# Attention with 49 agents and a maxout layer: a written-out order exchanged up to group 22, key values in pairs of chunks, five relu slots

## The chip, the cores and the metric

The kernel runs on one core of one Trainium2 chip. The metric is the time of one execution on the device, in microseconds (us), as the median of several runs. The core has five engines with an instruction stream each: PE (TensorE, matrix products), ACT (ScalarE), DVE (VectorE), POOL (GpSimd) and SP (SyncE, which here issues DMA transfers alone). Each works through its stream strictly in order. Transfers that SP issues form one queue, which sixteen DMA engines serve.

## The reference

Two layers follow each other. The first is attention through 49 agents: the agents gather from all keys and values of a batch, and each query then reads from the agents. The second is a maxout layer with three weight matrices and a product back to 128 columns.

```python
def _attn_ref(q, k, v, agents):          # q, k, v: 4 x 12544 x 128, agents: 4 x 49 x 128
    scale = 1.0 / np.sqrt(q.shape[-1])
    def sm(a, b):
        s = scale * (a @ b.transpose(0, 2, 1))
        ...
        return e / (e.sum(-1, keepdims=True) + 1e-09)
    a2k = sm(agents, k)
    agent_v = a2k @ v
    q2a = sm(q, agents)
    return q2a @ agent_v
def _moe_ref(x, w1, w2, w3, w_out):      # x: 50176 x 128, w1..w3: 128 x 768, w_out: 768 x 128
    h = np.maximum(np.maximum(x @ w1, x @ w2), x @ w3)
    return h @ w_out
```

## The kernel before, in words

**The algebra.** The output of the attention is never formed. For each batch the agents' values (49 x 128) are multiplied once by differences of the weights (w3-w1, w2-w1) and by w1 times w_out, into a table G of the batch (`gp`, `gv`). A row of the hidden layer then is a product of the 49 exponentials of a query with G, and the maximum of three becomes a relu of one difference (u), a maximum with the other (v), and a linear part (li) that goes straight to the output. The division by the sum of the exponentials comes last, when the output is scaled.

**Batches and groups.** There are 98 tiles of 128 rows per batch. Keys and values are taken in chunks of up to nine tiles (`chunks`, L175); queries in groups of eight tiles, 1024 rows: 12 groups a batch and one made of what remains, 49 in all (`parts_of`, L168). Batch 0's keys and values must be done before group 0, those of batch 1 before group 12, of batch 2 before group 24, of batch 3 before group 36. Chunks of the next batch are worked off between the groups.

**The steps**, by the names of the order (`graph`, L208):

- Chunk g of batch b: `kl`, `vl` load keys and values (SP), `kc`, `vc` cast them to bf16 (POOL; in batch 0 `vc` is on ACT), `kt` turns the keys (by PE and a copy `ke` on DVE in batch 0, by a transposing DMA on SP's queue later, L283), `ks` are the scores (PE, L285), `kx` the exponentials (ACT), `kv` the values (PE), `va` their sum (DVE), `ea` the sum of the exponentials (POOL).
- Group s: `ql` loads queries (SP), `qc` casts them (POOL). They are turned either by PE with a copy on DVE (`qt`, `qe`) or by a transposing DMA on SP's queue (`qd`); the list TURNED (L26) says which groups take the DMA (L318). `sc` are the scores (PE), `ex` the exponentials (ACT). For each of six parts f of the hidden layer: `u` (PE), `a` the relu (ACT), `v` (PE), `x` the maximum (DVE); for part 4 both are on ACT. `li` and `p` are the products into the output (PE; ROWS says for each part whether the 128 rows are taken as a whole or in two halves that run side by side), `su` and `re` the sums and their reciprocals, `ov` the scaling (DVE, or ACT where SCALER says so), `st` the store (SP).

**What sets the order.** No scheduler runs when the kernel is built. ORDER (L826) is a string of step names that was written out beforehand; `Emit.run` walks it once, and each engine's stream is its steps in that order. A number behind a name is the slot that a new tile takes in its pool (SLOTS, L46): 13 buffers for loads (LD), 3 each for cast queries and keys (QB, KB), 4 for turned ones (QT, KT), 3 for relus (AS), 13 for hidden parts (R), 10 for outputs (OS), 8 banks of PSUM (PS). `Plan.waits` works out from the order which step waits for which, a step that takes over a slot waiting for those that used it. All steps go through one recording helper, so that every row of the profile has that helper's line, L388; the rows are told apart by tile names.

Of the kernel before, what the change touches and what calls it, by code (L numbers as in the profile page):

```python
# [9 lines left out]
FP32 = mybir.dt.float32  # L10
# [9 lines left out]
C31, C21, C1O, WC = 0, DFF, 2 * DFF, 2 * DFF + C  # L20
CV, CT = KT * A, (KT - 1) * A
FI = 4
SPARE = 8
FIRST = [KT] * 10 + [4, 4]
LATER = [KT] * 10 + [8]
TURNED = (10, 13, 15, 18, 22, 24, 25, 28, 29, 30, 31, 32, 33, 34, 35, 36, 37, 38, 39, 40, 41, 42, 43, 44, 45, 46, 47, 48,)  # L26
ROWS = """
rrfrff rrrffr ffrfff ffrfrr rfffff rrrrrr ffffff ffffrr fffrff rfrrfr fffffr ffrfrf rrfrrr fffffr fffffr frffrf fffrrr rfffff
ffffff rrrfff ffffrf rrrfff rrffrr ffrrrr rrrrrr ffffff ffffff rrfffr ffrfrr rrrrrr ffffff ffffff fffffr rffrfr rrrrrr ffrffr
# [3 lines left out]
...... u..... .u.... ...... ...... ...... ...... ...... ...... ...... .u.u.. uu.... ...... ...... ...... ...u.. ..u... ......  # L33
...... ...... ...... .u.... ...... ...... ..u... ..u..u ...... ...... ...... ...... ..u... ...... ...... ...... ...... ......
...... ...... ...... ...... ...... ...... ...... ...... u..... ...... ...... ...... ......
""".split()
SCALER = """
dd dd dd dd dd dd dd dd dd dd dd dd dd dd dd dd dd dd dd dd dd dd ad dd dd dd dd dd dd dd dd dd dd dd dd dd dd dd dd dd dd dd dd
# [16 lines left out]
class Plan:  # L55
# [104 lines left out]
    def lane(self, o, place, first):  # L160
        if not o["use"]:
            return "AG"
# [45 lines left out]
def graph(plan, em):  # L208
# [3 lines left out]
    add("id0", POOL, em.clear_ident, (0.3, 0.6))  # L212
    add("id", POOL, em.make_ident, (0.3, 0.6), after=["id0"])
    add("ones", DVE, em.make_ones, (1.0, 1.1), after=["id0"])
    add("agl", ACT, em.load_agents, (0.5, 5.0), dma=True)
    add("agc", DVE, em.cast_agents, (0.42, 0.52), after=["agl"])
    add("agt", PE, em.turn_agents, (0.2, 0.4), after=["agc", "id"], new=[("PS", "agt")])
# [23 lines left out]
    for g in range(len(ch)):  # L241
        add(f"wn.{g}", PE, em.warm(f"warn.{g}", 2), (0.445, 0.67), after=["id", f"vl0.{g}"], new=[("PS", f"warn.{g}")])
# [812 lines left out]
```

## Time and profile before

| | |
|---|---|
| runs | 438.46, 439.33, 439.44 us (median 439.33) |
| profiled execution: span from first to last instruction | 436.6 us |
| PE busy | 411.9 us, 6488 matmuls |
| DVE busy | 386.6 us, 470 instructions |
| ACT busy | 393.9 us, 486 instructions |
| POOL busy | 170.0 us |
| moved by DMA | 122.37 MB, mean 280 GB/s |

The span starts with the first instruction of any engine. The runs' median is 2.7 us over the span; what lies around the span isn't in the profile. PE's busy time is modelled, since matmuls overlap in the array, and a busy PE isn't one at its peak. In a row of a window the busy times come in the order PE, PEld (loading of weights), DVE, ACT, POOL, then the clock granted to PE, the share of time that the sixteen DMA engines were at work (over 1 where packets overlap), and the rate. In rows for one tile a name stands for all buffers of its pool: QT is turned queries, KT turned keys, LD loads, R hidden parts, AS relus, VA sums of values, OS outputs, agT the agents. "DMA to landing" is from the start of SP's instruction to the arrival of the transfer's last completion.

### The profile page before, as it was taken

The page shows a single profiled execution, that of the slowest core. Times are in us where ns is not written, and L with a number is a line of the kernel's source. Part 1 is how long each engine was busy: PE and PEld are TensorE (multiplying, and loading weights), DVE is VectorE, ACT ScalarE, POOL GpSimd, SP SyncE. Part 2 cuts the span into 40 slices and gives each one's busy share as a digit, 9 for nine tenths or more (in the row PEclk, how much of TensorE's full clock was granted, in tenths as well). Part 3 has the DMA queues.
Part 4 walks back from the last instruction along what each step waited for, and adds up shares of the span by engine and source line. Part 5 has one row for each costly group of instructions (what it writes and reads, how often), then busy time and mean ns, then how long its engine had stood idle before and what let it go on. Part 6 is the DMA issues. An engine that isn't in the chain of part 4 may idle for free.

```text
span 436.6 us, 14853 instructions
## 1 busy us (share of the span) xinstructions
PE 411.9 (94%) x6488; PEld 256.9 (59%) x6488; DVE 386.6 (89%) x470; ACT 393.9 (90%) x486; POOL 170.0 (39%) x177
## 2 busy tenths in 40 slices
PE   1788999999999999999999999999999999999994
PEld 1464565666666566656656655656656555655574
DVE  1435999999999999999998999899999999999994
ACT  1278999999999999999999899999999999999993
POOL 3541565556655535165525445342531111000000
PEclk9989999999999999999999999999999999999999
DMA  8999999999999999999999999996999994266313
GB/s 310 411 410 383 311 334 372 289 281 343 269 318 342 279 371 298 266 339 285 294 345 261 407 247 278 276 326 143 276 363 290 284 306 98 74 208 208 119 71 125
DMA packets 98107, 122.37 MB, mean 280 GB/s; under 512 B 71479, under 2 KB 74235, under 8 KB 98043
## 3 DMA queue, kind: packets, MB, share of 16 engines
q1 hardware_dynamic: 97552, 121.07, 95.2%
q8 instruction: 51, 0.84, 0.8%
q10 hardware_dynamic: 491, 0.36, 0.3%
q14 instruction: 13, 0.11, 0.1%
HBM read 78.74 MB, written 25.69 MB: 239 GB/s over the span
## 4 chain that ended last, share of the span: by engine, by line
PE 69%; ACT 16%; DVE 7%; DMA 4%; issue 2%; POOL 1%; SPq 0%; POOLq 0%
PE ps L388 69%; ACT AS L388 9%; DVE R L388 6%; DMA LD<-in_k_dram 4%; ACT R L388 2%; ACT ps L388 2%; POOL KB L388 1%; DVE OS L388 1%; ACT EQ L388 1%; ACT VB L388 1%; ACT G L388 1%; ACT EK L388 1%; ACT OS L388 0%; SPq L388 0%; DVE QT L388 0%
## 5 line engine op out<-in xcount | busy, mean ns | idle before, releaser
L388 DVE TENSOR_TENSOR R<-ps,AS 128x1024 bf16<-128x1024 f32 x245 | 293.5, 1219 | 15.1 <-PE ps L388 10.7
L388 ACT ACTIVATE AS<-ps 128x1024 bf16<-128x1024 f32 (+1 forms) x259 | 245.8, 987 | 10.0 <-PE ps L388 7.2
L388 PE MATMUL ps<-EQ,G 49*128 49x512 bf16 (+1 forms) x1248 | 203.3, 370 | 3.5 <-ACT AS L388 0.7
L388 PE MATMUL ps<-wo_bf,R 64*128 64x128 bf16 (+1 forms) x3368 | 194.0, 218 | 1.1 <-issue 0.8
L388 PEld LDWEIGHTS ps<-wo_bf,R 64*128 64x128 bf16 (+1 forms) x3368 | 139.5, 95 | 59.4 <-issue 31.3
L388 PEld LDWEIGHTS ps<-EQ,G 49*128 49x128 bf16 x1248 | 56.4, 93 | 63.8 <-DVE R L388 18.3
L388 POOL CAST QB<-LD 128x1024 bf16<-128x1024 f32 x49 | 50.5, 1040 | 94.6 <-DMA QT<-QB 49.8
L388 POOL CAST KB<-LD 128x1152 bf16<-128x1152 f32 (+2 forms) x45 | 49.8, 1115 | 52.1 <-DMA LD<-in_k_dram 41.8
L388 DVE TENSOR_TENSOR OS<-ps,RC 128x512 f32<-128x512 f32 x96 | 65.4, 682 | 2.6 <-PE ps L388 2.2
L388 POOL CAST VB<-LD 128x1152 bf16<-128x1152 f32 (+1 forms) x33 | 37.4, 1136 | 40.7 <-DMA LD<-in_v_dram 36.5
L388 ACT ACTIVATE ps<-ps 128x1024 f32<-128x1024 f32 x49 | 49.9, 1018 | 2.8 <-PE ps L388 2.2
L388 ACT ACTIVATE R<-ps 128x1024 bf16<-128x1024 f32 x49 | 50.3, 1027 | 1.9 <-PE ps L388 1.6
L388 ACT ACTIVATE EK<-ps 128x441 bf16<-128x441 f32 (+2 forms) x45 | 23.4, 535 | 18.8 <-PE ps L388 18.4
L388 POOL TENSOR_TENSOR EA<-EA,EK 128x441 f32<-128x441 f32 x27 | 27.6, 1022 | 25.4 <-ACT EK L388 25.1
L388 ACT ACTIVATE EQ<-ps 128x512 bf16<-128x512 f32 x49 | 29.9, 610 | 1.0 <-PE ps L388 0.5
L388 DVE COPY KT<-ps 128x1152 bf16<-128x1152 bf16 (+1 forms) x12 | 8.2, 701 | 14.0 <-PE ps L388 14.0
L388 PE MATMUL ps<-QT,agT 128*64 128x512 bf16 (+1 forms) x104 | 19.9, 388 | 0.2
L388 PE MATMUL ps<-G,EQ 49*128 49x128 bf16 x392 | 19.1, 217 | 0.0
L388 PE MATMUL ps<-EK,VB 128*128 128x49 bf16 x392 | 17.4, 186 | 1.6 <-ACT VB L388 1.6
L388 PEld LDWEIGHTS ps<-EK,VB 128*128 128x128 bf16 x392 | 13.9, 97 | 8.1 <-ACT EK L388 4.2
L388 PE MATMUL ps<-agT,KT 128*128 128x49 bf16 x392 | 17.4, 186 | 0.4 <-DVE KT L388 0.4
L388 PEld LDWEIGHTS ps<-agT,KT 128*128 128x128 bf16 x392 | 14.4, 98 | 4.7 <-issue 2.1
(59 smaller groups left out, 177.6 us busy)
## 6 DMA issues: line engine op xcount, KB each, us to landing
LD<-in_q_dram SPq DMA_DIRECT2D x48, 512.0 KB, 7.7
out_dram<-OS SPq DMA_DIRECT2D x48, 512.0 KB, 6.2
LD<-in_k_dram SPq DMA_DIRECT2D x40, 576.0 KB, 7.6
LD<-in_v_dram SPq DMA_DIRECT2D x40, 576.0 KB, 8.4
LD<-in_k_dram SPq DMA_DIRECT2D x3, 512.0 KB, 5.3
LD<-in_v_dram SPq DMA_DIRECT2D x3, 512.0 KB, 6.7
LD<-in_moe_w_dram SPq DMA_DIRECT2D x6, 192.0 KB, 10.6
KT<-KB SPq DMA_TRANSPOSE x33, 7.3
```

The lines of the kernel that those rows point to most:

```text
L388: i = call(*args, **named)
```

## The change

- ORDER is another one up to group 22. From the middle of group 22's products on, the engines' streams are the old ones, with other slots; some casts and stores that stood behind the join stand ahead of it.
- Batch 0 is cut into twelve chunks of eight tiles and one of two, its values are loaded into output buffers and cast on ACT, POOL or DVE (VCAST), its exponentials lie in R slots, sums and values have a PSUM bank each. The weights' loads are cut into three parts each, and the products for G of batch 0 accordingly (CUTS, PARTS).
- The queries of groups 20, 21 and 23 are turned by DMA (TURNED).
- `u` can be evacuated in two halves as before, and now `v` too (SPLIT: u, v, or b for both). Up to group 22 there are 24 more halves of relus and 41 more of maxima than before.
- `kv` takes two chunks at a time into a bank of its own, and `va` adds once per pair.
- AS has five slots instead of three.
- The linear part of G has 256 columns, a half for each side, with zeros beside it, copied in two pieces. (LINEAR could take it in two products; it is "b" throughout, which is the old way.)

```diff
-FIRST = [KT] * 10 + [4, 4]
+FIRST = [GT] * 12 + [2]
-TURNED = (10, 13, 15, 18, 22, 24, 25, 28, 29, 30, ...
+TURNED = (10, 13, 15, 18, 20, 21, 22, 23, 24, 25, 28, 29, 30, ...
 SPLIT = """
-...... u..... .u.... ...... ...... ...... ...... ...... ...... ...... .u.u.. uu.... ...... ...... ...... ...u.. ..u... ......
+v.v..b vbvv.. v.u..v uv.... .....v uv.v.u ..v... .b.u.v v.vb.b .uuv.. uu.u.u vvb..v ..bv.u .....b ubv... .vbu.. uvb..v .v.b.u
...
-SLOTS = {"PS": 8, "LD": 13, "QB": 3, "KB": 3, "VB": 4, "KT": 4, "QT": 4, "EQ": 4, "EK": 4, "AS": 3,
+SLOTS = {"PS": 8, "LD": 13, "QB": 3, "KB": 3, "VB": 4, "KT": 4, "QT": 4, "EQ": 4, "EK": 4, "AS": 5,
...
-            add(f"kv{r}", PE, em.values(b, g, n, m), mm(n, 49), after=[f"kx{r}", f"vc{r}"], use=[m, f"vb{r}", f"e{r}"])
-            add(f"va{r}", DVE, em.add_values(b, g, m), (0.13, 0.25), after=[f"kv{r}"] + ([f"va{b}.{g - 1}"] if g else []),
-                use=[m, plan.tile("VA", f"va{b}")])
+            if g % 2 or g == len(ch) - 1:
+                two = [(x, ch[x][1]) for x in range(g // 2 * 2, g + 1)]
+                y, h = f"{b}.{g // 2}", f"y{b}.{g // 2}"
+                add(f"kv{y}", PE, em.values(b, two, h), mm(sum(x[1] for x in two), 49), after=[f"{z}{b}.{x}" for x, _ in two for z in ("kx", "vc")],
+                    new=[("PS", h)], use=[f"{z}{b}.{x}" for x, _ in two for z in ("vb", "e")])
+                add(f"va{y}", DVE, em.add_values(b, g // 2, h), (0.13, 0.25), after=[f"kv{y}"] + ([f"va{b}.{g // 2 - 1}"] if g > 1 else []),
+                    use=[h, plan.tile("VA", f"va{b}")])
...
+                if SPLIT[s][f] in "vb":
+                    vs = [f"{v}.{h}" for h in range(2)]
+                    add(v, PE, em.hidden(vs, s, f, C21, True), pe, mode=ROW, after=[f"ex.{s}"] + needs(1), new=[("PS", x) for x in vs],
+                        use=[e] + gs)
+                    for h in range(2):
+                        add(f"x.{s}.{f}.{h}", DVE, em.max_second(vs[h], s, f, h), (0.6, 0.72), after=[v, f"{a}.{h if SPLIT[s][f] == 'b' else 0}"],
+                            use=[vs[h], a, r])
```

ORDER itself is a table of some 2900 names; at three places its effect on the streams is shown. First SP's stream around the transposition for group 22, before. In it OS are stores, LD loads of q, k or v, QT turned queries, KT turned keys; from above, the QT row is group 22, the two KT rows chunks 9 and 10 of batch 2, the stores those of groups 9, 17 and 15.

```order
L388 DMA LD_88<-in_q_dram 128x1024
L388 DMA out_dram<-OS_143 128x1024
L388 DMA LD_84<-in_k_dram 128x1152
L388 DMA LD_82<-in_v_dram 128x1152
L388 DMA_TRANSPOSE KT_102<-KB_96 128x9x128
L388 DMA LD_80<-in_v_dram 128x1024
L388 DMA_TRANSPOSE QT_106<-QB_91 128x8x128
L388 DMA out_dram<-OS_144 128x1024
L388 DMA LD_85<-in_q_dram 128x1024
L388 DMA out_dram<-OS_140 128x1024
L388 DMA_TRANSPOSE KT_101<-KB_94 128x8x128
```

SP's stream at that place now: from above, the four QT rows are groups 20, 21, 22 and 23, the KT rows chunks 10, 7 and 9 of batch 2, the store that of group 4.

```order
L416 DMA LD_77<-in_v_dram 128x1152
L416 DMA_TRANSPOSE QT_101<-QB_88 128x8x128
L416 DMA_TRANSPOSE KT_97<-KB_91 128x8x128
L416 DMA_TRANSPOSE KT_99<-KB_92 128x9x128
L416 DMA_TRANSPOSE QT_104<-QB_87 128x8x128
L416 DMA_TRANSPOSE KT_98<-KB_90 128x9x128
L416 DMA_TRANSPOSE QT_102<-QB_89 128x8x128
L416 DMA_TRANSPOSE QT_103<-QB_88 128x8x128
L416 DMA LD_75<-in_v_dram 128x1152
L416 DMA out_dram<-OS_139 128x1024
```

Three of the four transposed query tiles are new on this queue; seven transpositions stand one behind another.

The second place is SP's stream at the store of group 1 (the row with OS_136 now). Before, that store (OS_141) stood behind the transposition of chunk 3.1 (the KT row on top).

```order
L388 DMA_TRANSPOSE KT_102<-KB_95 128x9x128
L388 DMA LD_84<-in_v_dram 128x1152
L388 DMA out_dram<-OS_143 128x1024
L388 DMA LD_90<-in_q_dram 128x1024
L388 DMA LD_85<-in_q_dram 128x1024
L388 DMA LD_83<-in_v_dram 128x1152
L388 DMA out_dram<-OS_141 128x1024
```

Now it stands between loads for batches 1 and 2 (group 15's queries on top, chunk 2.0's keys at the bottom). The store of group 13 moved too, from behind chunk 3.8's transposition to ahead of chunk 2.7's load of keys; all other stores that stood ahead of chunk 3.1's transposition still do.

```order
L416 DMA LD_77<-in_q_dram 128x1024
L416 DMA LD_78<-in_k_dram 128x1152
L416 DMA LD_76<-in_q_dram 128x1024
L416 DMA LD_81<-in_v_dram 128x1152
L416 DMA LD_79<-in_q_dram 128x1024
L416 DMA out_dram<-OS_136 128x1024
L416 DMA LD_80<-in_k_dram 128x1152
L416 DMA LD_83<-in_k_dram 128x1152
```

The third place is PE's stream at the scores of group 20 (the row with agT and QT). Before, the queries were turned by eight products with the unit matrix (ident) some rows ahead.

```order
L388 MATMUL ps<-ident,QB_93 128x128 x8
L388 MATMUL ps<-EK_114,VB_99 128x49 x9
L388 MATMUL ps<-wo_bf,R_121 128x128 x4
L388 MATMUL ps<-wo_bf,R_128 128x128 x4
L388 MATMUL ps<-EQ_112,G_148 128x512 x6
L388 MATMUL ps<-G_148,EQ_109 128x128 x8
L388 MATMUL ps<-wo_bf,R_128 128x128 x4
L388 MATMUL ps<-wo_bf,R_122 128x128 x8
L388 MATMUL ps<-EQ_112,G_148 128x512 x6
L388 MATMUL ps<-QT_105,agT 64x512 x2
```

Now no such row stands there, and the values (EK and VB) of two chunks follow each other.

```order
L416 MATMUL ps<-EK_112,VB_95 128x49 x9
L416 MATMUL ps<-EK_111,VB_93 128x49 x9
L416 MATMUL ps<-EQ_108,G_146 128x512 x2
L416 MATMUL ps<-G_146,EQ_107 128x128 x8
L416 MATMUL ps<-EQ_108,G_146 128x512 x2
L416 MATMUL ps<-wo_bf,R_126 128x128 x4
L416 MATMUL ps<-wo_bf,R_122 128x128 x4
L416 MATMUL ps<-wo_bf,R_127 128x128 x4
L416 MATMUL ps<-EQ_108,G_146 128x512 x4
L416 MATMUL ps<-wo_bf,R_122 128x128 x4
L416 MATMUL ps<-QT_101,agT 64x512 x2
```

PE and DVE lose the turning of groups 20, 21 and 23; the scores of group 25 stand behind the same products in both orders.

More of the change, by code (lines that the diff above doesn't have):

```diff
@@ L331, in graph, with needs @@
         for f in range(NF):
-            def needs(first, second):
+            def needs(second):
                 out = []
                 for p in parts:
-                    out.append(f"gv{first if f < 3 else second}" + (str(p[0]) if p[0] else ""))
+                    if p[0]:
+                        out.append(f"gv{'abcd'[second * 2 + f // 3]}{p[0]}")
+                    else:
+                        out.append(f"gv{'abcdef'[second * 3 + (f > 0) + (f > 2)]}0")
                 return out
-            e, u, v, r, two = f"e.{s}", f"u.{s}.{f}", f"v.{s}.{f}", plan.tile("R", f"r.{s}.{f}"), SPLIT[s][f] == "u"
+            e, u, v, r = f"e.{s}", f"u.{s}.{f}", f"v.{s}.{f}", plan.tile("R", f"r.{s}.{f}")
@@ new lines, in graph @@
+                add(f"a.{s}.{f}.0", ACT, em.relu(u, u, None), (0.917, 1.076), after=[u], use=[u])
+                add(v, PE, em.hidden([u], s, f, C21, False), pe, mode=ROW, after=[f"a.{s}.{f}.0"] + needs(1), use=[u, e] + gs)
+                if SPLIT[s][f] == "d":
+                    add(f"x.{s}.{f}.0", DVE, em.relu(r, u, None, DVE), (1.14, 1.28), after=[v], use=[u, r])
+                else:
+                    add(f"x.{s}.{f}.0", ACT, em.relu(r, u, None), (0.917, 1.076), after=[v], use=[u, r])
@@ L344, in graph @@
             else:
                 a = plan.tile("AS", f"a.{s}.{f}")
-                if two:
+                if SPLIT[s][f] in "ub":
                     us = [f"{u}.{h}" for h in range(2)]
-                    add(u, PE, em.hidden(us, s, f, C31, True), pe, mode=ROW, after=[f"ex.{s}"] + needs("a", "b"), new=[("PS", x) for x in us],
+                    add(u, PE, em.hidden(us, s, f, C31, True), pe, mode=ROW, after=[f"ex.{s}"] + needs(0), new=[("PS", x) for x in us],
                         use=[e] + gs)
@@ L352, in graph @@
                 else:
-                    add(u, PE, em.hidden([u], s, f, C31, True), pe, mode=ROW, after=[f"ex.{s}"] + needs("a", "b"), new=[("PS", u, 3)], use=[e] + gs)
-                    add(a, ACT, em.relu(a, u, None), (0.917, 1.076), after=[u], use=[u, a])
-                add(v, PE, em.hidden([v], s, f, C21, True), pe, mode=ROW, after=[f"ex.{s}"] + needs("c", "d"), new=[("PS", v, 3)], use=[e] + gs)
-                add(f"x.{s}.{f}", DVE, em.max_second(v, s, f), (1.14, 1.28), after=[v] + ([f"{a}.{h}" for h in range(2)] if two else [a]),
-                    use=[v, a, r])
@@ L358, in graph @@
-        lin = ["gvl" if p[0] == 0 else f"gvl{p[0]}" for p in parts]
+                    add(u, PE, em.hidden([u], s, f, C31, True), pe, mode=ROW, after=[f"ex.{s}"] + needs(0), new=[("PS", u, 3)], use=[e] + gs)
+                    add(f"{a}.0", ACT, em.relu(a, u, None), (0.917, 1.076), after=[u], use=[u, a])
+                if SPLIT[s][f] in "vb":
[5 more added lines that the diff above has]
+                            use=[vs[h], a, r])
+                else:
+                    add(v, PE, em.hidden([v], s, f, C21, True), pe, mode=ROW, after=[f"ex.{s}"] + needs(1), new=[("PS", v, 3)], use=[e] + gs)
+                    add(f"x.{s}.{f}.0", DVE, em.max_second(v, s, f, None), (1.14, 1.28), after=[v] + [f"{a}.{h}" for h in range(1 + (SPLIT[s][f] == "u"))],
+                        use=[v, a, r])
@@ L463, in clear_ident, with clear_linear @@
         self.nc.gpsimd.memset(self.sides, 0.0)
+    def clear_linear(self):
+        for i in range(SLOTS["G"]):
+            self.nc.gpsimd.memset(self.slots["G", i][:, C1O:], 0.0)
     def make_ident(self):
```

644 lines of the change are left out of this document (341 added, 303 removed).

## The prediction

> **What bounds the kernel now.** I read the page's slices first (part 2), where all four of PE, DVE, ACT and DMA look full, then the groups, then stretches by window, then single transfers. The first view is the page's slices of 10.9 us each: busy tenths of DVE and ACT, the granted clock, the DMA engines' share and the rate.
>
> ```profile
> DVE  1435999999999999999998999899999999999994
> ACT  1278999999999999999999899999999999999993
> DMA  8999999999999999999999999996999994266313
> GB/s 310 411 410 383 311 334 372 289 281 343 269 318 342 279 371 298 266 339 285 294 345 261 407 247 278 276 326 143 276 363 290 284 306 98 74 208 208 119 71 125
> ```
>
> From slice 4 to slice 34 ACT and DVE stand at nine tenths, and so do the DMA engines, though the rate wanders between 143 and 411 GB/s. A queue that is full at 300 GB/s has something in it that is not measured in bytes. Three windows show what: the first two hold one query transposition each, the third plain loads.
>
> ```profile
> 255.00:257.20 2.20, 2.20 (x26) 1.14 (x24) 2.20 (x5) 2.05 (x3) 2.20 (x3) 1.00 1.14 136
> 288.10:290.30 2.20, 2.20 (x60) 1.64 (x56) 2.20 (x3) 2.06 (x3) 0.32 (x1) 1.00 1.36 131
> 107.00:109.30 2.30, 2.30 (x22) 1.02 (x22) 2.19 (x3) 2.30 (x4) 2.02 (x2) 1.00 1.04 410
> ```
>
> The columns are PE, PEld, DVE, ACT and POOL busy time, clock, DMA share and GB/s. While a transposition runs, the sixteen engines are over 100% busy and move 131 to 136 GB/s, 0.29 to 0.30 MB in 2.2 us; the tile itself is 128x1024 bf16, 0.26 MB, so 0.03 to 0.04 MB (0.1 us at 410) is other traffic: 2.1 us for one, in which almost nothing else moves. A load or store of 128x1024 f32 (0.524 MB) costs 0.524/0.410 = 1.28 us.
>
> A long stretch checks both prices: the number of transpositions issued between 60 and 280 us (by tile name), and the window over the same time.
>
> ```profile
> L388 SPq DMA_TRANSPOSE KT<-KB x28: 1248/2811/6979, 59.3 to 275.9; - x28
> L388 SPq DMA_TRANSPOSE QT<-QB x11: 1237/2894/6058, 102.6 to 272.8; - x11
> 60.00:280.00 220.00, 218.75 (x3444) 136.42 (x3438) 208.87 (x253) 209.74 (x262) 116.57 (x118) 1.00 1.11 309
> ```
>
> 220 us at 309 GB/s are 68.0 MB. The 39 transposed tiles hold about 11.1 MB of it (0.29 MB a key tile, 0.26 a query tile). The other 56.9 MB take 138.8 us at 410; 81.2 us are left for 39 transpositions, 2.08 each. Both prices hold together only if the DMA engines had no pause in 220 us, and their share of 1.11 says the same. So up to 280 us a transfer lands when the work ahead of it on SP's queue is done, and anything added ahead makes it later, one for one. DVE and ACT have 11.1 and 10.3 us of idle time in those 220 us.
>
> What the engines lose by this is read from single transfers: issue (last times of the row), issue to landing, and the first matmul that reads the tile on PE. First group 25's queries.
>
> ```profile
> L388 SPq DMA_TRANSPOSE QT<-QB x1: 6058/6058/6058, 221.8 to 221.8; - x1
> DMA to landing us min/median/max: 12.1/12.1/12.1
> ...
> L388 PE MATMUL ps<-QT,agT x2: 403/403/403, 237.6 to 237.6; 128*64 128x512 bf16 x2
> ```
>
> Landed at 233.9, read at 237.6: 3.7 us to spare. Then chunk 1 of batch 3's keys, chunk 0 of batch 2's, and chunk 9 of batch 3's.
>
> ```profile
> L388 SPq DMA_TRANSPOSE KT<-KB x1: 3035/3035/3035, 233.0 to 233.0; - x1
> DMA to landing us min/median/max: 6.2/6.2/6.2
> ...
> L388 PE MATMUL ps<-agT,KT x9: 183/183/197, 242.9 to 243.2; 128*128 128x49 bf16 x9
> ```
>
> ```profile
> L388 SPq DMA_TRANSPOSE KT<-KB x1: 2497/2497/2497, 116.5 to 116.5; - x1
> DMA to landing us min/median/max: 7.7/7.7/7.7
> ...
> L388 PE MATMUL ps<-agT,KT x8: 183/183/197, 134.5 to 134.7; 128*128 128x49 bf16 x8
> ```
>
> ```profile
> L388 SPq DMA_TRANSPOSE KT<-KB x1: 1445/1445/1445, 300.5 to 300.5; - x1
> DMA to landing us min/median/max: 3.2/3.2/3.2
> ...
> L388 PE MATMUL ps<-agT,KT x9: 183/183/187, 306.8 to 307.0; 128*128 128x49 bf16 x9
> ```
>
> To spare: 242.9-239.2 = 3.7 us, 134.5-124.2 = 10.3, 306.8-303.7 = 3.1. The queue does not show in the chain of waits because the order leaves these few microseconds; it is the second bound, 3.7 us behind the compute engines at groups 24 and 25.
>
> **The change, part by part.** The sum goes against the profiled span, 436.6 us; the median of the runs is 439.33, so 2.7 us lie around the span.
>
> *Three more transpositions, and stores that go ahead.* The queries of groups 20, 21 and 23 leave PE and DVE for SP's queue: 3 x 2.1 = 6.3 us of queue. In the order, the stores of groups 1 and 13 now stand before the transposition for group 25 and that for chunk 3.1; before they stood behind both: 2 x 1.28 = 2.6 us. All else ahead of these two places is the same loads, in bytes. So both land 8.9 us later: 242.8 and 248.1 instead of 233.9 and 239.2. Less the 3.7 us to spare, PE meets them 5.2 us later than before, whatever the engines did until then. PE takes its instructions in order: behind the scores of group 25 (sc.25) stand the hidden layer of group 24 and the output of 23, on these ACT and DVE wait, and on them the rest of the program, which keeps its old order. The price of one query transposition lies between 1.9 (the 81.2 us shared out by tile size, a query tile being 8/9 of a key tile) and 2.3 (the whole 2.2 us of a window and a tenth for the hand-over); I take 2.1, what the windows give: 5.2 becomes 4.6 to 5.8 at the ends.
>
> The other places: ahead of chunk 2.0 stand five key and value loads (0.59 MB each) and one query load that stood behind it: 3.5 MB, 8.5 us, so it lands at 132.7 where it was read at 134.5. So already in group 11 the new order cannot be more than 1.8 us ahead of the old one. At chunk 3.9 only the three transpositions remain: 6.3-3.1 = 3.2 us late, less than the 5.2 already lost.
>
> *Start.* The last values of batch 0 and their cast on ACT:
>
> ```profile
> L388 SPq DMA_DIRECT2D LD<-in_v_dram x2: 432/432/432, 27.2 to 27.6; - x2
> ...
> DMA to landing us min/median/max: 9.4/9.9/10.4
> ...
> 38.47 1.16 ACT L388 ACTIVATE VB<-LD 128x1152 bf16<-128x1152 f32 x1
> ```
>
> They land at 27.6+10.4 = 38.0 and ACT casts them 0.4 us later. The new order has the same 12.8 MB and one q load ahead of them at the same rate, and casts on POOL, ACT and DVE. Gain: 0.5 us, between 0 and 1.5 (the cast and the 0.3 us for the weights' first part). It is gone at chunk 2.0.
>
> *Work of ACT and DVE up to group 22.* The rows for it, from the groups by shape:
>
> ```profile
> L388 DVE TENSOR_TENSOR R<-ps,AS 128x1024 bf16<-128x1024 f32 x245 | 293.5, 1219 | 15.1 <-PE ps L388 10.7 <-ACT AS L388 1.2
> L388 ACT ACTIVATE AS<-ps 128x1024 bf16<-128x1024 f32 x231 | 230.9, 1033 | 7.8 <-PE ps L388 5.2
> L388 DVE TENSOR_TENSOR OS<-ps,RC 128x512 f32<-128x512 f32 x96 | 65.4, 682 | 2.6 <-PE ps L388 2.2
> L388 ACT ACTIVATE AS<-ps 128x512 bf16<-128x512 f32 x28 | 15.4, 604 | 2.2 <-PE ps L388 2.0
> L388 DVE COPY QT<-ps 128x1024 bf16<-128x1024 bf16 x21 | 14.3, 683 | 1.4 <-PE ps L388 1.4
> L388 DVE TENSOR_TENSOR VA<-ps,VA 128x49 f32<-128x49 f32 x30 | 5.9, 197 | 0.3
> ```
>
> ACT splits 24 more relus in two: 24 x (2 x 0.604-1.033) = +4.2 us. DVE splits 41 maxima; the nearest row for a half is the 128x512 product at 0.682: 41 x (1.364-1.219) = +5.9; it loses three evacuations (-2.0) and ten sums of values, by pairs (-2.0). So +4 on ACT, +2 on DVE, against idle time of 11.1 and 10.3 us in 220, or 9.1 and 8.4 in the 180 us from 60 to 240: -8 to +4 in all, and I take 0, because the queue decides first. The halves free PSUM banks sooner; ACT's row shows its waits ended by PE, not by DVE, so five relu slots instead of three take away nothing that stands there: 0.
>
> *Behind group 22* the engines' order is the old one. A typical stretch there:
>
> ```profile
> 320.00:360.00 40.00, 39.29 (x640) 23.36 (x638) 38.91 (x44) 39.16 (x47) 8.27 (x8) 1.00 1.12 304
> ```
>
> DVE and ACT are 97 and 98% busy, so lost time isn't won back. Five sums of values go (5 x 0.197 = 1.0 us on DVE), the linear part is copied in two pieces: 0, at most -1.5.
>
> Sum: 436.6+5.2 = 441.8 of span, with 2.7 around it **444.5 us**.
>
> [...]
>
> **The rivals.** *Faster: the order pays and the queue gives way.* Half of DVE's and ACT's idle time from 60 to 240 us goes (9.1 and 8.4, so -4.4), and the start gives -0.5: 439.3-4.9 = 434.4. It decides if the transfer for group 25 lands before 229, which needs room in the queue that the share of 1.11 denies; for it speaks that landing times were read in one execution. Chance 0.13.
>
> *Much slower: the stop costs clock.* Two stretches of the start show what a waiting PE does.
>
> ```profile
> 24.00:28.00 4.00, 2.36 (x51) 2.04 (x49) 0.51 (x2) 2.64 (x4) 2.10 (x2) 0.88 1.02 408
> 28.00:32.00 4.00, 4.00 (x53) 2.75 (x51) 1.23 (x3) 2.70 (x6) 1.56 (x3) 0.69 1.03 413
> ```
>
> PE was busy for 59% of four microseconds, and the clock fell to 0.88 and 0.69. The same after the stops at groups 24 and 25 would take (0.12+0.31) x 4 = 1.7 us each, 3.4: 447.9, and a little more if the queue also runs dry behind a wait. PE is not the tightest engine, which speaks against. Chance 0.17. [...]
>
> *No change: a transposition costs its bytes.* Beside other transfers it would then take 0.26/0.41 = 0.64 us, three 1.9, with the stores 4.5, less 3.7 to spare: 0.8 late, 440.1. The 81.2 us left over for 39 of them speak against it. Chance 0.07.
>
> **How the numbers follow.** The forecast has 0.63 and reaches from 442 to 447: 4.6 to 5.8, less 1.5 or plus up to 1.5 for the split work. Faster has 0.13, no change 0.07, slower 0.63+0.17 = 0.80; 0.2% (0.9 us) is about what the measurement can tell. The range reaches down over the no-change case to 440 and up to 449; outside lie the faster case and the far end of the slowest.
>
> **What would show it.** In the new profile: sc.25 and the keys of chunk 3.1 read some 243 and 248 us from the start, right at their landing, with PE, ACT and DVE idle ahead of them and the idle time put down to a DMA into QT or KT; DMA share still above 1 up to there. The forecast is wrong if these are read before 238, or if they land that late and the end still comes by 440.

## The result, and the profile after

| | median | lowest to highest | runs |
|---|---|---|---|
| after | 440.85 us | 438.87 to 443.53 | 6 |
| before, beside it | 438.41 us | 437.85 to 439.44 | 6 |

The ratio is 1.0052, 95% interval [1.0031, 1.0074]: slower by 2.4 us, where 5.2 were forecast. The profiled execution took 440.69 us; its span is 438.6. First the page's slices, as those shown of before.

```profile
DVE  1434999999999999999899999899999999999994
ACT  1255999998999999999999899999999999999994
DMA  7999999999999999999999989999699992256313
GB/s 274 413 410 374 306 291 378 240 412 234 356 396 215 348 410 257 345 259 290 417 313 294 387 238 271 286 261 269 203 335 274 320 277 74 75 160 239 134 60 136
```

Counted from 0, no slice of DVE or ACT from 4 to 38 falls under eight tenths: the stop that was forecast for slices 21 and 22 (230 to 252 us) isn't there. Next two single transfers on which the forecast stood: first the queries of group 25 in the profile of after, their issue, landing and first matmul.

```profile
L416 SPq DMA_TRANSPOSE QT<-QB x1: 3107/3107/3107, 226.6 to 226.6; - x1
...
DMA to landing us min/median/max: 8.3/8.3/8.3
...
L416 PE MATMUL ps<-QT,agT x2: 403/403/403, 238.6 to 238.6; 128*64 128x512 bf16 x2
```

They landed at 226.6+8.3 = 234.9 and were read 3.7 us later. Chunk 1 of batch 3's keys, in the same way:

```profile
L416 SPq DMA_TRANSPOSE KT<-KB x1: 2820/2820/2820, 234.7 to 234.7; - x1
...
DMA to landing us min/median/max: 6.3/6.3/6.3
...
L416 PE MATMUL ps<-agT,KT x9: 183/183/198, 243.9 to 244.1; 128*128 128x49 bf16 x9
```

Landed at 241.0, read at 243.9, 2.9 us to spare. So two landings that were to come 8.9 us later came 1.0 and 1.7 us later, and nothing waited for them. (Chunk 2.0 landed at 133.9 and was read 1.2 us later.)

The same stretch of the queue, from 45 us to the landing of group 25's queries, in before and in after:

```profile
45.00:234.00 189.00, 187.59 (x2932) 116.53 (x2932) 180.38 (x221) 180.55 (x226) 101.89 (x103) 1.00 1.11 312
```

```profile
45.00:235.00 190.00, 187.44 (x2856) 115.35 (x2855) 182.21 (x253) 182.81 (x255) 102.46 (x105) 1.00 1.09 321
```

In practically the same time the new order moved 321x190 = 61.0 MB instead of 312x189 = 59.0, three transpositions more among them, at a smaller share of busy engines. Where the time came from shows in the packets. A transposition is carried in packets of 256 bytes, 18 ns each at the median (66304 of them in before, 17.0 MB, as much as its 61 transposed tiles). Some of them take 0.3 to 1.5 us (a few up to 2.3), many at once, and end together; meanwhile little or nothing moves. Below I say that such packets stand. Two such stretches of before, the second with the microsecond ahead of it:

```profile
76.65:78.10 1.45, 1.45 (x38) 1.00 (x32) 1.08 (x3) 1.45 (x3) 1.11 (x2) 1.00 1.01 32
254.90:255.90 1.00, 1.00 (x12) 0.39 (x8) 1.00 (x4) 0.85 (x2) 1.00 (x2) 1.00 2.12 270
255.90:257.20 1.30, 1.30 (x18) 0.85 (x18) 1.30 (x2) 1.30 (x2) 1.30 (x2) 1.00 0.35 34
```

The first has a share of 1.01 and 32 GB/s: the engines count as busy, and stand. A window counts a packet's time where the packet begins, so the packets that stand from 255.9 on are in the share of 2.12 ahead of it. Both windows that priced a transposition at 2.1 us in the prediction hold such a stand, 0.8 us from 255.9 and 1.3 us from 288.6. I took from the trace, for the same stretch, the time in which at least 14 packets moved at once (there are 16 engines), and that in which fewer than 8 did:

```
                  until landing   moving   between   standing (us)
before                   233.9     156.1       4.4       28.3
after                    234.9     163.7       5.6       20.6
```

The work that was added is there, 7.6 us of moving more (8.9 were forecast); but 7.7 us of standing are gone.

Where the 2.4 us come from instead: starts of the first u of some groups against the profile of before, in the profiles of after and of a second set of runs of it (e5, below).

```
               before    after   after again
group 0         41.41    +0.79      -0.66
group 9        113.68    +2.39      +1.26
group 21       212.90    +0.61      -0.82
group 24       238.05    +1.06      -0.36
group 37       339.93    +2.23      +0.82
```

The two profiles differ by 1.4 us from the start, by the landing of batch 0's last values (39.5 and 38.0 us). From group 0 to 24 both lose 0.3 (what they lose up to group 9 they win back by 21); from 24 to 37, behind the join at group 22 from which the order is the old one, both lose 1.2.

### The profile page after: what moved, and what is told of

The parts are those of the page before. It is cut to its first block, busy times and chain, and to the rows that moved or that the text cites. A ratio compares the mean times of both kernels' runs of the same rounds, so it can differ in the third digit from the quotient of the medians.

```text
span 438.6 us, 14798 instructions
## 1 busy us (share of the span) xinstructions
PE 415.3 (95%) x6428; PEld 257.0 (59%) x6428; DVE 386.6 (88%) x498; ACT 390.7 (89%) x511; POOL 176.5 (40%) x188
## 4 chain that ended last, share of the span: by engine, by line
PE 54%; ACT 17%; DMA 10%; DVE 6%; POOL 5%; SPq 4%; issue 3%; POOLq 0%; DVEq 0%
PE ps L416 54%; ACT AS L416 10%; DVE R L416 4%; DMA LD<-in_k_dram 4%; SPq L416 4%; DMA LD<-in_q_dram 3%; ACT R L416 3%; ACT ps L416 2%; DMA LD<-in_moe_w_dram 2%; POOL KB L416 2%; DMA KT<-KB 1%; ACT EQ L416 1%; POOL QB L416 1%; POOL VB L416 1%; POOL EA L416 1%
## 5 line engine op out<-in xcount | busy, mean ns | idle before, releaser
L416 DVE TENSOR_TENSOR R<-ps,AS 128x1024 bf16<-128x1024 f32 (+1 forms) x286 | 296.0, 1065 | 14.2 <-PE ps L416 9.1
L416 ACT ACTIVATE R<-ps 128x1024 bf16<-128x1024 f32 (+1 forms) x58 | 54.8, 946 | 19.3 <-PE ps L416 19.0
L416 DVE TENSOR_TENSOR OS<-ps,RC 128x512 f32<-128x512 f32 x95 | 64.5, 682 | 2.5 <-PE ps L416 1.9
L416 ACT ACTIVATE EK<-ps 128x441 bf16<-128x441 f32 (+2 forms) x37 | 19.6, 535 | 5.0 <-PE ps L416 4.8
L416 DVE COPY KT<-ps 128x1024 bf16<-128x1024 bf16 (+1 forms) x13 | 8.1, 657 | 13.4 <-PE ps L416 13.4
L416 PEld LDWEIGHTS ps<-G,EQ 49*128 49x128 bf16 x392 | 13.7, 94 | 4.6 <-ACT EQ L416 0.5
L416 PE MATMUL ps<-ident 128*128 128x512 bf16 x47 | 13.8, 404 | 1.8 <-POOL ident L416 1.6
```

The lines of the kernel that those rows point to most:

```text
L416: i = call(*args, **named)
```

## The experiments

Ratios are to before on the same chip. "Offset" is the start of a step against the profile of before.

**e1: the queue alone.** No engine computes: seven stretches of loads (L, 0.52 MB) and transposed query tiles (T, 0.26 MB), each waiting for the one ahead.

```diff
+SECTIONS = ("L" * 24, "T" * 12, "LLT" * 12, "LLLLTT" * 6, "LLLLLLTTT" * 4, ("L" * 12 + "T" * 6) * 2, "L" * 24 + "T" * 12)
```

> No computation: only SP's queue, in seven sections, each waited for before the next (L is a load of 128x1024 f32, T a transposition of a 128x1024 bf16 tile): 24 L; 12 T; 12 x LLT; 6 x LLLLTT; 4 x LLLLLLTTT; 2 x (12 L, 6 T); 24 L and then 12 T. The output is left out but for one store. Theory of the runs (a transposition behind another costs less than one between loads, about 1.5 us against 2.1 to 2.4): the third section takes 24 x 1.28 + 12 x 2.3 = 58 us, the sixth and seventh about 31 + 12 x 1.5 = 49, those between them in between. Rival, the prediction's price (2.1 us wherever it stands): the last five sections are alike, 56 us each. [...]

From first issue to last landing: 34.1, 18.3, 44.8, 51.9, 50.1, 49.7 and 48.8 us. Windows of e1 inside the first three stretches (POOL busy, clock, share, GB/s):

```profile
6.00:34.00 28.00, 0.00 (x0) 1.00 1.02 406
40.00:53.00 13.00, 0.00 (x0) 1.00 1.01 191
58.00:98.00 40.00, 0.00 (x0) 1.00 1.09 367
```

One T among loads adds (44.8-34.1)/12 = 0.89 us, in runs of two and three 1.48 and 1.33; back to back SP issues one per 1.38 us. So runs of transpositions are not cheaper, against the theory that the new order saves by them; a flat 2.1 falls too, and so does the price by bytes (0.64, the prediction's third rival).

**e2: batch 3's values singly again.** In after, every chunk of batch 3 has its own values and sum, as before.

```diff
-            if g % 2 or g == len(ch) - 1:
+            if b == 3:
+                add(f"kv{r}", PE, em.values_there(b, g, n, m), mm(n, 49), after=[f"kx{r}", f"vc{r}"], use=[m, f"vb{r}", f"e{r}"])
...
+            elif g % 2 or g == len(ch) - 1:
```

> The changed kernel, but batch 3's values by single chunks again, in the bank of the chunk's scores and at the old places behind the join. Theory of the pairs (each pair of chunks holds PE up for 0.23 us longer at a place where ACT and DVE wait for it): the 1.2 us that are lost between groups 24 and 37 go to 0.3 or less, 439.7 us or 1.0025 of the time before. Rival (slots, stores or the linear part's two pieces lose it): no change, 1.005.

438.34 us, 0.9996 [0.9982, 1.0010]. The loss is gone, and more than was expected of it. In the profiles after loses 1.4 us from group 26 to 37 and e2 0.6. As a median e2 lies 2.5 us below after; 0.8 of that is seen in the profiles.

**e3: the transpositions apart.** After, with loads drawn between neighbouring transpositions, so that 33 of them stand in 33 runs.

```diff
-kl2.9/4 ... kt2.7/2
+kt2.7/2 ... kl2.9/4
```

> The changed kernel with a load or store between any two of the 33 transpositions ahead of group 25's scores: 22 loads and stores stand some places later on SP's queue, nothing else moves, and the work ahead of the transposition for group 25 is the same. Theory of the runs: 33 runs of one instead of 11 runs cost 22 x 0.5 = 11 us more of queue, the transposition for group 25 lands at about 246 instead of 234.9 us, its scores are read then, and the time is 445 to 449 us. Rival (the price does not depend on the neighbours; the queue had room all along): it lands at 235 to 236, and the time stays at 441.

458.34 us, 1.0448 [1.0428, 1.0467], which neither theory gave. Three windows of e3:

```profile
120.00:140.00 20.00, 20.00 (x299) 12.70 (x295) 19.72 (x30) 19.08 (x29) 10.08 (x13) 1.00 0.74 184
140.00:160.00 20.00, 15.05 (x192) 8.68 (x191) 13.35 (x18) 12.78 (x19) 6.78 (x8) 0.83 0.92 239
200.00:220.00 20.00, 9.82 (x144) 6.53 (x142) 8.27 (x13) 8.53 (x13) 7.04 (x7) 0.75 1.08 271
```

The queue ran dry first (share 0.74), then PE, DVE and ACT waited. In the kernel a transposition waits for the cast of its tile, and SP's stream stands with it: between 120 and 230 us SP waited 13.4 us for POOL's casts of keys (KB, four times, the longest 7.3), and chunk 2.9's load stood behind 2.7's transposition. The DMA engines had nothing at all to do for 12.2 us up to the landing of group 25's queries at 252.4. Apart from that they stood for 24.6 us, less than in before although every run was of one: against the theory that runs save.

**e4: only three transpositions more.** Before, with groups 20, 21 and 23 turned by DMA, each right behind its cast.

```diff
-TURNED = (10, 13, 15, 18, 22, 24, 25, 28, 29, 30, ...
+TURNED = (10, 13, 15, 18, 20, 21, 22, 23, 24, 25, 28, 29, 30, ...
```

> The kernel before with the queries of groups 20, 21 and 23 turned by DMA, each right behind its cast, and nothing else changed: the first stands alone between two loads, the second and third beside a transposition that was there. Prediction's price, 3 x 2.1 us: the transposition for group 25 lands at 240.2 instead of 233.9, 2.6 us after it was read: 441 us, 1.006. Theory of the runs: one alone at 2.3 and two in runs at 1.5 are 5.3 us, it lands at 239.2, 1.6 late: 440, 1.003. Rival (the queue had room): it lands by 237 and DVE is spared 2.0 us of copies: 437 to 438.4, 0.997 to 1.000.

441.17 us, 1.0063 [1.0048, 1.0077]. The queries of group 25 landed at 236.3, 2.4 us later than before; the stop came earlier. Group 23's own tile landed at 222.87 and was read at 222.91. Windows of e4 there, and of before:

```profile
222.00:224.00 2.00, 1.39 (x8) 0.27 (x7) 1.62 (x2) 1.08 (x2) 1.41 (x2) 0.66 1.20 273
224.00:226.00 2.00, 2.00 (x22) 1.09 (x20) 1.23 (x1) 1.21 (x2) 0.00 (x0) 0.50 0.95 367
226.00:228.00 2.00, 2.00 (x32) 1.45 (x28) 1.08 (x1) 1.26 (x2) 0.00 (x0) 0.50 1.03 404
```

```profile
222.00:224.00 2.00, 2.00 (x23) 1.08 (x22) 2.00 (x4) 2.00 (x4) 0.00 (x0) 1.00 1.05 408
```

PE was idle for 0.6 us of the first two and for as long in the two ahead of them, and the granted clock fell to 0.50 for the four after. Group 23's first u went from -0.78 to +2.61. From there to the end the offset stayed at +2.4: lost time isn't won back.

**e5: after again**, as it is, to see how far its median and its profile move.

> The changed kernel itself, unchanged, to have it on the same chip as the next three: 1.003 to 1.007 of the time before by every theory.

440.79 us, 1.0047 [1.0029, 1.0065].

**e6: halves taken whole.** After, with 31 evacuations in one piece that the change had split.

```diff
-v.v..b vbvv.. v.u..v uv.... .....v uv.v.u ..v... .b.u.v v.vb.b .uuv.. uu.u.u vvb..v ..bv.u .....b ubv... .vbu.. uvb..v .v.b.u
+v.v..v vb.v.. ..u..v uv.... ...... .v...u ...... .u.u.. ..vb.v .uu... ...u.u ..b..v ...v.. .....v .b.... .vbu.. u.v..v .....u
```

> The changed kernel with 31 of its split evacuations up to group 22 taken as one instruction again, at the place of the first half: the 15 relus and 16 maxima whose two PSUM banks lie side by side, so that no slot changes. Theory of the work (ACT and DVE have no room, so the split costs what it takes): 15 x 0.175 = 2.6 us less on ACT and 16 x 0.145 = 2.3 on DVE, of which 1 to 2.3 show in the time: 0.995 to 0.998 of the changed kernel. Rival (a half frees its bank sooner and so pays for itself): 1.000 to 1.004 of it. The prediction's value, 0: no change.

446.29 us, 1.0169 [1.0147, 1.0192]: 5.5 us slower than after, lost between groups 7 and 13 (+1.5 to +6.0). Windows of e6 and of after:

```profile
60.00:120.00 60.00, 57.42 (x920) 35.87 (x915) 55.40 (x68) 54.64 (x70) 32.94 (x33) 1.00 1.12 309
```

```profile
60.00:120.00 60.00, 59.31 (x959) 37.48 (x955) 57.54 (x79) 56.70 (x76) 34.20 (x33) 1.00 1.09 310
```

With whole pieces PE, DVE and ACT are each busy for 2 us less of the 60. That a bank held for a whole piece keeps PE back is how I read it; the runs show the loss, not its way. The halves pay for their work in this order.

**e7: chunk 1.7 earlier.** In after, chunk 1.7 landed 0.05 us ahead of its read; here its load stands ahead of 1.9's and its transposition ahead of four loads.

```diff
-kl1.9/7 kl1.8/8 kl1.7/6 ... vl1.6/11 vl1.8/10 kl1.10/0 ql.12/1 kt1.7/3
+kl1.7/7 kl1.8/8 kl1.9/6 ... kt1.7/3 vl1.6/11 vl1.8/10 kl1.10/0 ql.12/1
```

> The changed kernel with chunk 7 of batch 1 ahead of chunk 9 on SP's and POOL's queues, and its transposition ahead of five loads (values, keys, queries): in the changed kernel its scores are read at 105.0 us, 0.05 us after the keys have landed. Theory of an early queue (the new order is held up there, and what is lost isn't won back): the keys land at about 100, the scores are read 1 to 2 us sooner, and the time is 0.5 to 1.5 us less, 0.997 to 0.999 of the changed kernel. Rival (ACT and DVE set the pace there, and the new order wins back the 1.8 us between groups 9 and 21 anyway): no change.

442.51 us, 1.0083 [1.0060, 1.0107]. Chunk 1.7 came 4.9 us ahead of its read, and group 9 started at +0.40 instead of +2.39 (+1.26 in e5). But the queue was no faster: PE reached groups 24 and 25 earlier, and there the transfers were late. The chain of waits of e7:

```profile
236.31 7.94 DMA KT<-KB
244.25 0.14 issue
244.38 3.64 PE ps L416 x45
```

Chunk 3.1 landed at 244.25 and was read at once; 3.3 us were lost at groups 24 and 25. That is the prediction's place and mechanism: after stands on the other side of it, with 3.7 and 2.9 us to spare (2.3 and 1.5 in e5).

**e8: e2 with the linear part in one piece.**

```diff
-            cuts = [(src, out)] if c0 < C1O else [(src[h * H:(h + 1) * H, :], self.t[f"G{b}"][h * H:(h + 1) * H, c0 + h * C:c1 + h * C]) for h in range(2)]
+            cuts = [(src, out)]
```

> The kernel with batch 3's values singly, and with the linear part of G copied in one piece, as before, for all batches. Theory: behind the join the last 0.6 us of the loss go (between groups 33 and 37, at batch 3's G), and some 0.2 us at each of batches 1 and 2: 0.6 to 1 us less than with the values singly alone, 437.5 us or 0.998 of the time before. Rival (the copies are hidden): no change to that, 438.4.

439.44 us, 1.0018 [1.0001, 1.0035]. From e2 that can't be told apart: the two pieces cost nothing that shows. Under after it lies 1.4 us with both edits, where e2 had 2.5 with one of them, so by medians the price of batch 3's pairs is known to about 1 us only.

**e9: the queue beside busy engines.** Eight times LLT with nothing beside it, with 42 copies on POOL, on DVE, on ACT, and on all; then 16 loads and 8 T, and 16 loads alone.

```diff
+SECTIONS = (("LLT" * 8, ""), ("LLT" * 8, "p"), ("LLT" * 8, "d"), ("LLT" * 8, "a"), ("LLT" * 8, "pda"), ("L" * 16 + "T" * 8, "pda"), ("L" * 16, "pda"))
```

> No computation of the reference: SP's queue again, this time beside engines that cast 128x1024 tiles from f32 to bf16 in SBUF all the time. Seven sections, each waited for: 8 x LLT with no engine at work; the same beside POOL, beside DVE, beside ACT, beside all three; 16 L and then 8 T beside all three; 16 L beside all three. The output is left out but for one store. Theory of contention (the engines' traffic in SBUF makes a transposition dear, 0.9 us in the queue alone against 2.1 in the kernel): a section beside the engines takes 8 x 1 = 8 us or more longer than the first (about 31 us), and the packets of the transpositions take 30 ns or more on average instead of 18 to 22. Rival (it is the order and the moments of issue, not the engines): all the LLT sections are alike within 2 us.

31.2, 30.9, 31.0, 31.5, 30.7, 33.5, 23.3 us: a T costs 0.9 to 1.0 among loads, whichever of these three computes beside it, and 1.27 behind them. The traffic of POOL, DVE and ACT isn't what makes the packets stand; PE did nothing here.

**e10: after with groups 20, 21 and 23 on PE again.**

```diff
-TURNED = (10, 13, 15, 18, 20, 21, 22, 23, 24, 25, 28, 29, 30, ...
+TURNED = (10, 13, 15, 18, 22, 24, 25, 28, 29, 30, ...
```

> The changed kernel with the queries of groups 20, 21 and 23 turned by PE and copied by DVE again, nine steps of PE ahead of their scores. The prediction's price, 3 x 2.1 us: the transposition for group 25 lands 6.3 us earlier than in the changed kernel (its two profiles have 234.9), at 228 to 229. Theory of cheap transpositions in a run (1.5 us or less each, some of it in pauses): 2 to 4.5 us earlier, 230.5 to 233. In the time both expect no gain from the queue, which has 2 to 4 us to spare there, and up to 2.0 us more work on DVE: 440.8 to 443, 1.005 to 1.010 of the time before.

449.52 us, 1.0254 [1.0234, 1.0273]. A miss: 6 us were lost at groups 19 to 23, as I read it because this order had no room for three more PSUM banks and copies (between 190 and 240 us PE's weight loads waited 2.2 us for QB and 1.6 for QT), and so it says nothing of the queue.

**e11: pairs pulled apart in batches 1 and 2**, on e8: the first chunk's products some steps earlier into the same bank, for seven of ten pairs.

```diff
-                add(f"kv{y}", PE, em.values(b, two, h), mm(sum(x[1] for x in two), 49), ...
+                for i, (x, k) in enumerate(two):
+                    add(f"kv{y}" if i == len(two) - 1 else f"kv{y}f", PE, em.values(b, [(x, k)], h, i), mm(k, 49), ...
```

> The kernel with batch 3's values singly and the linear part in one piece, and in seven of the ten pairs of batches 1 and 2 the first chunk's values three to six steps of PE ahead of the second's, into the same bank. Theory of the pairs (18 products in a row hold ACT and DVE up by 0.23 us each): 7 x 0.23 = 1.6 us less, 438 us or less, 0.997 to 0.999 of the time before. Rival (up to group 22 the order was made for the pairs, and their wait is hidden): no change to the kernel that it starts from, 1.000 to 1.003.

446.50 us, 1.0186 [1.0167, 1.0204]. A miss too: the loss lies at groups 5 to 17, where a bank is now held for some steps longer.

**e12: issue and fetch.** Eight times a T and three loads: SP issues the next T when the one ahead and the load behind that have landed, or already when the one ahead begins; then both beside 700 products on PE, which read the tile that is transposed.

```diff
+SECTIONS = (("after", False), ("during", False), ("after", True), ("during", True))
```

> No computation of the reference: SP's queue with eight units of one transposition and three loads in each of four sections. In the first and third SP issues the next transposition after the running one has landed, in the second and fourth when the running one begins; in the third and fourth PE works through 700 small products at the same time, so that instructions are fetched. The output is left out but for one store. In the kernel before, packets of transpositions stood still for 28 us in all between 45 and 234 us, mostly when SP took up another transposition or a 16 KB packet of instructions was under way. Theory of the issue: the second section stands 1 us or more at each of six transpositions, 6 to 8 us longer than the first. Theory of the fetch: the third is longer than the first by 1.4 us at each of the packets of instructions that meet a transposition, 2 to 5 us in all, and the second is not. Rival (neither, something else of the kernel): all four are alike within 1.5 us.

Windows of e12, one inside each stretch (PE, PEld, POOL, clock, share, GB/s):

```profile
2.00:49.00 47.00, 0.00 (x0) 0.00 (x0) 0.00 (x0) 1.00 1.01 312
49.20:90.80 41.60, 1.08 (x11) 1.11 (x12) 0.00 (x0) 1.00 1.01 353
91.00:141.90 50.90, 40.34 (x690) 40.16 (x687) 0.00 (x0) 0.94 1.02 290
142.00:191.00 49.00, 41.10 (x700) 40.93 (x700) 0.00 (x0) 0.92 1.07 302
```

47.3, 41.7, 51.0 and 49.4 us. Issuing a T while another runs is cheaper, not dearer, so SP's issue alone isn't what stops the packets. Beside PE's products both cost more, by 3.8 and 7.8 us: fewer than 8 packets moved for 2.1 and 0.4 us in the first two stretches and for 4.8 and 6.2 us in the others. Of the 4.8 us, 3.0 lie beside a 16 KB packet that fetches instructions; of the 6.2 us, among them four stands of 1.4 us, none do. So beside PE's products packets stand without a fetch too, in this one execution.

**e13: e4 with group 23's queries in time**: their load, cast and transposition ahead of those of 24 and 25.

```diff
-ql.24/7 ... qc.24/1 ... ql.25/11 ... ql.23/1 ... qc.25/0 ... qc.23/2 qd.23/2 ... qd.24/3
+ql.23/7 ... qc.23/1 ... ql.24/11 ... ql.25/1 ... qc.24/0 ... qd.23/2 ... qc.25/2 ... qd.24/3
```

> The kernel before with the queries of groups 20, 21 and 23 turned by DMA as in the run with three by DMA, but group 23's queries change places with those of groups 24 and 25 on SP's and POOL's queues, so that they are there in time (there they landed as they were read, and that stop was the whole loss). Prediction's price, 6.3 us more of queue: the transposition for group 25 lands at 240 and is read 2.6 us late: 441 us, 1.006. Theory of the standing packets (the queue has 28 us in which its packets stand still, and three more transpositions go into that): it lands at 235 to 237 and is read on time, within 0.5 us: 437 to 438.5 us, 0.997 to 1.000.

441.12 us, 1.0055 [1.0034, 1.0076]. The tile now came 3.4 us ahead of its read, and the stop stayed. Windows of e13:

```profile
220.00:222.00 2.00, 0.98 (x6) 0.19 (x4) 1.60 (x3) 2.00 (x4) 1.84 (x4) 1.00 1.14 344
222.00:224.00 2.00, 1.49 (x14) 0.76 (x14) 0.68 (x2) 0.89 (x1) 1.92 (x4) 0.73 1.10 352
224.00:226.00 2.00, 2.00 (x18) 0.79 (x18) 2.00 (x2) 1.33 (x2) 0.54 (x1) 0.50 1.07 327
```

POOL is full there. Chunk 3.0's values landed 3 us later than before, POOL's cast of them waited, and behind it stood the folding of batch 2's sums (fo2), on which PE waits for batch 2's G. A later queue struck through a third engine.

**e14: only the pairs.** Before, with batch 3's first ten chunks in pairs at after's places.

```diff
+            if b < 3 or g == len(ch) - 1:
...
+            elif g % 2:
+                two = [(x, ch[x][1]) for x in range(g // 2 * 2, g + 1)]
...
+                    new=[("PS", h)], use=[f"{z}{b}.{x}" for x, _ in two for z in ("vb", "e")])
```

> The kernel before with the values of batch 3's first ten chunks in pairs, each pair in a bank of its own and at the places that the changed kernel gives it; nothing else differs. Theory of the pairs (0.23 us at each, ACT and DVE waiting for PE): 5 x 0.23 = 1.1 us more, 439.5 us, 1.002 to 1.003. Rival (the loss behind the join comes from the slots, the stores or the linear part): no change, 1.000.

440.39 us, 1.0041 [1.0025, 1.0057]: the pairs cost 1.8 us by themselves. In its profile 1.9 us are lost behind the join (offset +0.77 at group 26, +2.62 at 34); the 1.2 us that this profile also loses from group 0 to 12, where it does what before does, can't come from the edit. The costliest pair in e14's order of time (start, duration, what, idle before it), then the same place in before:

```profile
261.94 0.62 PE L396 MATMUL ps<-EK,VB 128*128 128x49 bf16 x18 [0.23 <-DVE R L396]
262.84 0.20 DVE L396 TENSOR_TENSOR VA<-ps,VA 128x49 f32<-128x49 f32 x1
263.10 0.39 PE L396 MATMUL ps<-EQ,G 49*128 49x512 bf16 x2 [0.54 <-DVE VA L396]
263.53 1.02 ACT L396 ACTIVATE AS<-ps 128x1024 bf16<-128x1024 f32 x1 [1.25 <-PE ps L396]
```

```profile
260.77 0.40 PE L388 MATMUL ps<-EK,VB 128*128 128x49 bf16 x9
261.10 0.39 PE L388 MATMUL ps<-EQ,G 49*128 49x512 bf16 x2
261.53 1.02 ACT L388 ACTIVATE AS<-ps 128x1024 bf16<-128x1024 f32 x1
```

A pair needs a PSUM bank of its own. PE waits 0.23 us for one, then its next product waits 0.54 us until DVE's sum has given one back, and ACT stands 1.25 us. Single values lie in the bank that the chunk already has. In after, the slots spare this pair most of it (0.23 us here), and another shows it:

```profile
278.39 0.64 PE L416 MATMUL ps<-EK,VB 128*128 128x49 bf16 x18
...
279.49 0.11 PEld L416 LDWEIGHTS ps<-QT,agT 128*64 128x64 bf16 x2 [0.42 <-DVE VA L416]
```

**e15: e13 with the folding ahead of the cast**, to take POOL's chain out.

```diff
-vc3.0/1 a.21.2/2 x.21.3/0 fo2.0 ... fo2.1 ... fo2.2 ... fo2/0
+fo2.0 fo2.1 fo2.2 fo2/0 vc3.0/1 a.21.2/2 x.21.3/0
```

> The kernel with three in time, and the four folding steps of batch 2 ahead of chunk 3.0's cast of values on POOL. Theory of the chain over POOL (the queue's delay was met there first, and the stop cost clock): the total of batch 2 no longer waits, PE doesn't stop at 221 us, the granted clock stays at 1.00, and the time is 437 to 438.7 us, 0.996 to 1.001. Rival, the prediction's place (groups 24 and 25 wait for their own tiles): 440 to 441, 1.004 to 1.006.

441.13 us, 1.0056 [1.0034, 1.0079]. Groups 23 and 24 were in time (+0.46), and the stop moved to the place that the prediction names: the queries of group 25 landed at 237.8 and were read 0.2 us later. The chain of waits of e15, and its windows:

```profile
237.44 8.41 DMA KT<-KB
245.85 0.14 issue
245.99 4.41 PE ps L388 x46
```

```profile
244.00:246.00 2.00, 0.01 (x1) 0.04 (x2) 1.58 (x2) 0.00 (x0) 0.00 (x0) 1.00 0.99 348
246.00:248.00 2.00, 2.00 (x25) 1.07 (x25) 0.41 (x1) 1.55 (x2) 0.81 (x1) 0.81 1.02 415
248.00:250.00 2.00, 2.00 (x27) 1.55 (x27) 1.09 (x3) 1.43 (x2) 0.63 (x2) 0.50 1.04 428
```

PE, in order, stood for all of 244 to 246 for chunk 3.1; 3.6 us were lost from group 24 to 25.

**e16: before with the folding ahead alone**, the control for e15 (same edit, on before).

> The kernel before with the same four folding steps ahead of chunk 3.0's cast of values on POOL, and nothing else. All theories: within 0.3 us of the kernel before, 0.999 to 1.001, since the total was not waited for there; if it gains more than that, what the run beside it gains is not the transpositions' room but the folding.

438.50 us, 0.9999 [0.9990, 1.0008]: the move itself does nothing.

The account of moving and standing once more (e3, e6, e10 and e11 are left out, since their engines or their queue were late for reasons of their own):

```
                               landed at   moving   standing (us)
old order (before, e14, e16)    230.7-233.9       156     26.3-28.3
old order + 3 (e4, e13, e15)    236.3-237.8   159-161     27.2-29.6
new order (after, e2, e5, e7, e8)             161-164     20.6-23.7
```

The column "between" of the table above makes up the rest of each stretch. In the old order three transpositions add 3.6 us of moving on average and 0.8 of standing, and the landing comes 5.0 us later (237.3 against 232.2): 1.7 us each. The standing that vanished goes with the new order, in all five kernels of this table that have it.

## Why the prediction was wrong, point by point

- **The queue, the step that failed.** "Both prices hold together only if the DMA engines had no pause in 220 us, and their share of 1.11 says the same", hence "so both land 8.9 us later". The share counts packets that stand (1.01 at 32 GB/s from 76.65 us), and the two windows that gave 2.1 us each hold a stand. Of the 2.1 us that were charged for each transposition, 1.2 is moving (3.6 us for three in the table above) and some 0.9 (28.3 us over the 30 of that stretch) is standing, which isn't bound to a transposition's count: after has three more and 0.6 each. The tenth for a hand-over in the upper price of 2.3 was my estimate; no run shows it. The 8.9 us of added work were nearly right (7.6), the rule "one for one" wasn't: 7.7 us of pauses went at the same time, the landing came 1.0 us later, and the 3.7 us to spare were still 3.7 when PE read (2.3 in e5). The reads at 238.6 and 243.9 lie just behind the 238 that the prediction named as its own test, yet PE waited for neither tile.
- **The mechanism behind it** was right where nothing gave way. In the old order (e15) three transpositions, at 1.7 us each instead of 2.1, make group 25 late by 3.6 us at that place, where PE waits for chunk 3.1; e7 puts after itself there. "Lost time isn't won back" held in e4.
- **Behind group 22**, "0, at most -1.5", had the wrong sign: 1.2 us lost in both profiles of after. e14 shows the pairs to cost 1.8 us where they stand alone, and e2 that after without batch 3's pairs equals before. I had counted DVE's five sums saved and not the bank that a pair takes. By the medians (2.5 us in e2, 1.4 in e8) this is the larger part of the 2.4 us; the profiles show 0.8 of it. The other 0.6 us of the loss behind the join, from group 34 to 37, are in e2 too, 0.3 in e8 and none in e14, so they aren't the pairs'; what they are wasn't separated.
- **Start.** The chain from the last values to the first u took 2.7 us instead of 3.4, the 0.5 that was forecast; but the values landed 0.8 us later on average (nine profiles with the new order, six with the old), so that nothing is left of it.
- **Work of ACT and DVE**, taken as 0: 0.3 us lost from group 0 to 24, start and queue included. What was behind the 0 wasn't right: the halves were given nothing for freeing banks sooner, and e6 puts 31 of them at 5.5 us in this order, in a way that the runs don't show.
- **Baseline.** 439.33 was the median of three; the runs beside after give 438.41. A run of before lies some 1.8 us above its own span and one of after 2.0 to 2.2, not 2.7, which set a median against the span of another execution. That took 0.9 us from the forecast's height.
- **Rivals.** The stop that costs clock was seen (0.50 in e4, e13 and e15, each time behind a stop of PE), but after has no such stop: from 230 to 252 us its PE is busy for 21.7 of 22 us and the clock is 1.00. The price by bytes isn't reached even in the queue alone (0.89 against 0.64), though that case's time, 440.1, is nearest to the result, by another way. The faster case needed a landing before 229, and it came at 234.9; the pairs stood against it, and perhaps chunks 1.0, 1.2 and 1.7, which in after are read 0.05 to 0.16 us after landing.
- **Open**: what makes packets stand, and what in the new order makes fewer of them. Tried and refuted are runs of transpositions (e1, e3), the traffic of POOL, DVE and ACT (e9) and SP's issue alone (e12). Instruction fetch fits 3.0 of the 11.0 us of standing beside PE's products in e12; in before 4 of 23 stands begin 0.45 to 0.6 us after a 16 KB fetch begins, and end some 0.8 us after it ends. Beside no such fetch lie 19 of the 23 in before and 9 of 15 in after, so it is these that the new order has fewer of. Also open is why e2 and after differ by 2.5 us as medians and by 0.8 in the profiles behind the join.

## What to carry to other kernels

A busy share over 1 on a DMA queue wasn't proof here that it had no slack (1.11, with 28 of 189 us standing): set the bytes beside it in windows of one or two microseconds, and look whether packets move, before a price per transfer is multiplied by a count. Where values are put together to save an instruction, count what they hold as well, here a PSUM bank until DVE has given it back (0.54 us of waiting in e14). A few microseconds of queue showed up wherever an engine in order waited first (group 23's tile in e4, POOL's cast in e13, chunk 3.1 in e15), so look at each tile's landing against its read, not only at the one with the least to spare.

## What the runs showed of the hardware

- Packets of 256 bytes, 18 ns each at the median, stood for some 1.4 us at a time, many at once, and counted as busy: 28 of 189 us in before.
- A transposed tile of 0.26 MB cost 0.9 us among loads with nothing else running (e1), 1.38 back to back, about SP's time for one (1.32 to 1.35); in this kernel 1.2 of moving, and 1.7 for one more in the old order (e4, e13, e15).
- After 1.2 to 2.5 us without work on PE within four the granted clock went to 0.50 for at least 2 to 4 us (e4: 1.2 of 220 to 224; e13: 1.5 of 220 to 224; e15: 2.5 of 242 to 246).
- A stream of 700 products on PE, which read the tile that is transposed, lengthened a queue of transpositions and loads by 8 to 19% in one execution (e12: 47.3 to 51.0, 41.7 to 49.4).
